# Attention with a routed MLP on one core: the last 20 score steps taken two at a time

## The chip, the cores and the metric

The kernel runs on one core of a Trainium2 chip. The metric is the device time of one execution in microseconds (us). The kernel before took 1442.85 us (median of 3 runs, 1442.76 to 1443.87).

## What is computed

```python
x = A_x                                              # 1 x 2048 x 512
g = sigmoid((x * gate_w).sum(-1, keepdims=True))
# a: 32 heads of 16 channels over 2048 tokens
q, k, v = heads(x @ wqkv)
p = softmax(q @ k.T * 16 ** -0.5)
a = merge(p @ v) @ wo
# b: the 2 tokens with the highest r = B_x @ w_r go through a SwiGLU MLP, times sigmoid(r), added to B_x
b = B_x + scatter(sigmoid(r_sel) * ((silu(x_sel @ w_gate) * (x_sel @ w_up)) @ w_down))
out = g * a + (1 - g) * b
```

Nearly all the work is the attention: 32 heads, each with a 2048 x 2048 score matrix.

## The kernel before, in words

**Units and steps.** The heads are taken in 16 pairs, and each pair in two halves of the queries (1024 each): 32 units. A unit goes through the 2048 keys in 16 blocks of 128, so there are 512 steps (`STEPS`). One step computes, transposed, the scores of 128 keys against 1024 queries for two heads: four *pieces* of S^T of 128 x 512, each one matmul into one PSUM bank (`s_piece`, L624), followed by an exp on ScalarE that writes a quarter of the SBUF tile `P` (L625). Which head a piece belongs to is `j` (rows 64 j and up of the K and Q tiles, 50 rows each), which half of the queries is `c`. The block P V of a step (`av_mm`, L633) is four column tiles of 32 accumulating into the one bank `av`; each of its four matmuls runs as two, so the trace shows eight. P V of step s - 2 is issued behind the pieces of step s. The tile `P` has three buffers.

**PSUM.** Eight banks: `st` (three, taken in rotation), `fl` (one), `mxa` (one tile of two banks), `mxb` (one), `av` (one). During the main part `mxa` and `mxb` hold the products from which VectorE takes row maxima (`m_piece`, L556 and L560). These run out before the steps do, and the last 20 steps (492 to 511) are driven by a plain loop, L922 to L930. There, the fourth piece of a step (c = 1, j = 0) goes to `mxb` and the other three to `st`.

**What the plain loop issues for a step.** `run_late`; the four pieces with their exps; P V of step s - 2; one entry of the generator `fills`; then `end_step(s)`, which runs what is due at that step in the table `fill`. Every engine takes its instructions in the order in which they are issued here. Two kinds of due work matter:

- *Output products* (`wo_last`, L534): three matmuls of 512 columns into the bank `fl` (L481), then `finish` on VectorE (L529), which reads `fl` and adds into `acc`. Products 8 to 15 (tokens of the second half, 96 rows) come from `fills` at steps 497 to 504, products 0 to 5 (128 rows, followed by a store to HBM, L532) from `end_step` at steps 506 to 511.
- *Pieces of the last heads' normalisation*: `n_last` (GpSimd, L679), `split_last` (cast on VectorE L524, subtraction on GpSimd L525) at steps 494, 495, 503 and 504; `l_cols` at 498 and `l_rows` at 499 (PE into `mxa`, L684 and L693, with VectorE L686, L688 and L695 behind them), `last_rows` at 500 (four DMAs, L700). Product 8 needs the first result of `split_last` of the second half, product 0 that of the first half.

P V of step 495 ends unit 30, whose sum VectorE copies out of `av` (L644). Steps 512 and 513 issue P V of 510 and 511 only. Then comes `tail`: the last unit's normalisation, its output products and the last ten stores.

Of the kernel before, what the change touches and what calls it, by code (L numbers as in the profile page):

```python
# [10 lines left out]
AF = mybir.ActivationFunctionType  # L11
# [9 lines left out]
KT = S // 128  # L21
VW = DH + 1
LEAD = 21
STEPS = UNITS * KT
# [9 lines left out]
def gated_mix(ctx: ExitStack, tc: tile.TileContext, xT, x, wqkv, wo, w_rg, w_gate, w_up, w_down,  # L34
              consts, pos, out):
    nc = tc.nc
# [10 lines left out]
    def st_tile(shape=(128, 512)):  # L47
        return psum.tile(list(shape), F32, tag="st", name="st", bufs=3)
# [4 lines left out]
    def mxa_tile():  # L53
        return psum.tile([128, 2, 512], F32, tag="mxa", name="mxa", bufs=1)

    def mxb_tile(shape=(128, 512)):
        return psum.tile(list(shape), F32, tag="mxb", name="mxb", bufs=1)
# [119 lines left out]
    def run_late():  # L177
        for f, a in late:
            f(*a)
        late.clear()  # L180
# [57 lines left out]
    def load_k(pair):  # L238

        g, r = divmod(pair * 32, 128)  # L240
        for j in range(2):
            o = (g * 128 + r + 16 * j) * S
            t = Kx[pair % 2].bitcast(F32)
            nc.sync.dma_start(t[64 * j:64 * j + 32, :], ap(qk_scr["k"], o, [[S, 16], [D * S, 2], [1, S]]).bitcast(F32))
            nc.sync.dma_start(t[64 * j + 32:64 * j + 48, :], ap(qk_scr["k"], o, [[S, 16], [1, S]]).bitcast(F32))

    def load_q(u):

        pair, half = divmod(u, 2)
        g, r = divmod(pair * 32, 128)  # L250
        n = S // 2
        for j in range(2):
            o = (g * 128 + r + 16 * j) * S + half * n
            t = Qx[u % 3].bitcast(F32)
            nc.sync.dma_start(t[64 * j:64 * j + 32, :], ap(qk_scr["q"], o, [[S, 16], [0, 2], [1, n]]).bitcast(F32))
            nc.sync.dma_start(t[64 * j + 32:64 * j + 48, :], ap(qk_scr["q"], D * S + o, [[S, 16], [1, n]]).bitcast(F32))
# [287 lines left out]
    MX, P, AV = {}, {}, {}  # L544
# [69 lines left out]
                p0 = 32 * b + 16 * j  # L614
                nc.sync.dma_start(q[:, :, 32 * b:32 * b + 32].bitcast(F32), r[p0:p0 + 16, :].bitcast(F32))  # L615

    def s_piece(s, j, c):
        u, kt = divmod(s, KT)
        if s not in P:
            P[s] = ring.tile([128, 4, 512], F32, tag="P", name="P", bufs=3)  # L620
        k = Kx[(u // 2) % 2][64 * j:64 * j + 50, kt * 128:kt * 128 + 128]
        q = Qx[u % 3][64 * j:64 * j + 50, c * 512:c * 512 + 512]
        ps = mxb_tile() if s > STEPS - LEAD and c == 1 and j == 0 else st_tile()
        nc.tensor.matmul(ps, k, q, start=True, stop=True)  # L624
        nc.scalar.activation(P[s][:, 2 * j + c, :], ps, AF.Exp)  # L625

    def av_mm(s):
        u, kt = divmod(s, KT)
        if kt == 0:
            AV[0] = av_tile()  # L630
        for ct in range(4):
            h = (u // 2) * 2 + ct // 2
            nc.tensor.matmul(AV[0][32 * ct:32 * ct + 32, :], V[:, kt, h * VW:h * VW + 32], P[s][:, ct, :],  # L633
                             start=kt == 0, stop=kt == KT - 1)
        del P[s]
# [3 lines left out]
    def av_out(u):  # L639
        pair, half = divmod(u, 2)  # L640
        g, pp = divmod(pair, 4)
        o = o_tile("o", [128, 512])
        if STEPS > u * KT + KT + 2 > STEPS - LEAD:
            nc.vector.tensor_copy(o, AV[0])  # L644
        else:
            nc.scalar.activation(o, AV[0], AF.Copy)
        if pair == PAIRS - 1:
            AV[u] = o
            return
        if u % 8 == 0:  # L650
            Lt[g] = ring.tile([128, 128], F32, tag="Lt", name="Lt", bufs=1)
        for ct in range(4):
            j, c = divmod(ct, 2)
            q0 = c * 512
            r = pp * 32 + j * 16
            if g < 3:
                d = a_scr[g * 128 + r:g * 128 + r + 16, half * 1024 + q0:half * 1024 + q0 + 512]
            else:
                d = last_n[half][r:r + 16, q0:q0 + 512]
            nc.sync.dma_start(d, o[32 * ct:32 * ct + 16, :])  # L660
            p = r + half * 8 + c * 4
            nc.sync.dma_start(Lt[g][p:p + 4, :], o[32 * ct + 16:32 * ct + 17, :])
# [91 lines left out]
    fill, now = {}, [0]  # L754

    def at_step(s, f, *a):
        fill.setdefault(s, []).append((f, a))

    def end_step(s):
        now[0] = s  # L760
        for f, a in fill.pop(s, []):
            f(*a)
# [28 lines left out]
    def slots():  # L791
        for w, nb in order:
            yield from proj(1, w, nb, 3)
        late.append((split_w, (2,)))
        at_step(now[0] + 4, load_w, 3)
        x_rows()
        yield
        for w, nb in order:
            yield from proj(2, w, nb, 3)
        for n, (w, nb) in enumerate(order):  # L800
            yield from proj(3, w, nb, 3)
            if w == "q":
                for i in range(4):
                    at_step(now[0] + i + 1, load_ff, ("gate", "up")[i // 2], (w_gate, w_up)[i // 2],
                            ("xh", "xl")[i // 2], nb, i % 2)
        yield from ff_in("gate")
        for j in range(4):
            at_step(now[0] + 2 * j, load_down, j)
        ff_t(0, "gate")
        yield  # L810
        yield from ff_in("up")
        ff_t(1, "up")
        late.append((ff_act, ()))
        at_step(now[0] + 3, ff_h)
        at_step(now[0] + 3, load_wo)
        for c in range(4):
            at_step(now[0] + 6 + c, split_wo, c)
        yield
        yield
        yield from ff_down()  # L820
        ff_sum()
        last_tiles()
        s = now[0]
        for nb in range(4):
            at_step(s + 5 + 2 * nb, load_acc, nb)
        for t in range(16):
            at_step(s + 11 + t, acc_scale, t)
        at_step(s + 1, load_at, 0, (0, 1))
        at_step(s + 4, split_at, 0, (0, 1))
        yield from wait(s + 8)  # L830
        yield from wo_groups((0, 1), (2,))
        assert now[0] > 3 * 8 * KT + 16
        yield from wo_groups((2,))
        yield from wait(STEPS - 15)
        for t in range(8, 16):
            wo_last(t, 96)
            yield

    fills = slots()
# [8 lines left out]
    def p_v(s):  # L848
        if not 0 <= s < STEPS:
            return  # L850
        av_mm(s)
        if s % KT < KT - 1:
            return
        u, s = s // KT, now[0]
        av_out(u)
        if u % 8 == 7 and u < 24:
            for i in range(8):
                at_step(s + 6 + i, l_out, u // 8, i)
        elif u == UNITS - 3:
            for i in range(8):  # L860
                at_step(s + 3 + i // 2, l_out, 3, i)
            for half in (1, 0):
                for q in range(2):
                    at_step(s + 10 - half, l_last, half, q)
                    at_step(s + 12 - half, n_last, half, q)
        elif u == UNITS - 2:
            at_step(s + 1, l_cols, u)
            at_step(s + 2, l_rows, u)
            at_step(s + 3, last_rows)

    def start_step(s):
        now[0] = s
        u = s // KT + 2
        if s % KT == 0 and u < UNITS:
            if u % 2 == 0 and u > 2:
                load_k(u // 2)
            load_q(u)

    count = dict(s=0, m=0, A=-2)
# [22 lines left out]
    while count["m"] < UNITS * EL:  # L902
        run_late()
        for o in ORDER:
            if o == "s":
                s, i = divmod(count["s"], 4)
                if i == 0:
                    start_step(s)
                s_piece(s, i % 2, i // 2)
                count["s"] += 1  # L910
                if i == 3:
                    end_step(s)
            elif o == "m":
                m_next()
            elif o == "A":
                if count["A"] < 0:
                    parts_next(3)
                p_v(count["A"])
                count["A"] += 1
            else:  # L920
                next(fills, None)
    for s in range(count["s"] // 4, STEPS + 2):  # L922
        run_late()
        if s < STEPS:
            start_step(s)
            for i in range(4):
                s_piece(s, 1 - i % 2, i // 2)
        p_v(s - 2)
        next(fills, None)
        end_step(s)  # L930
    end_step(STEPS + 2)
    assert next(parts, 0) == 0 and not fill and next(fills, 0) == 0, fill
    tail()
# [31 lines left out]
```

## Time and profile before

| | us |
|---|---|
| median of the runs | 1442.85 |
| the profiled execution | 1443.71 |
| its span, first to last instruction | 1441.9 |
| PE busy / VectorE busy / ScalarE busy / GpSimd busy | 1426.5 / 1300.1 / 1168.7 / 302.5 |
| start of step 492, the first of the plain loop | 1372.76 |
| start of the last two P V blocks | 1424.41 |

A row of the timeline gives the start in the span, the length, the engine, the source line, the operation with out<-in, shapes and count (neighbours of one kind are merged), and in brackets how long the engine had been idle and who released it. PEld is the load of the stationary operand, which runs beside PE's matmuls. Matmul lengths contain the latency of the array, so the distance between starts tells what a matmul costs in a stream.

### The profile page before, as it was taken

How to read it: one execution, taken by the hardware profiler on the slowest of the kernel's cores; microseconds unless marked ns; L12 is line 12 of the kernel's file. 1: busy time of each engine (PE TensorE's matmuls, PEld its weight loads, DVE VectorE, ACT ScalarE, POOL GpSimd, SP SyncE). 2: the span in 40 equal slices, each digit the busy share in tenths (PEclk: the TensorE clock that was granted, in tenths of full speed). 3: DMA queues.
4: the chain of work that ended last, by engine and by line, in shares of the span. 5: the costliest groups of instructions: out<-in, count | busy, mean ns of one | idle time of the engine just before them, and what ended most of it. 6: DMA issues, size and time to landing. Idle time of an engine off the chain costs nothing.

```text
span 1441.9 us, 24169 instructions
## 1 busy us (share of the span) xinstructions
PE 1426.5 (99%) x9141; PEld 631.9 (44%) x9141; DVE 1300.1 (90%) x1541; ACT 1168.7 (81%) x2262; POOL 302.5 (21%) x321
## 2 busy tenths in 40 slices
PE   8999999999999999999999999999999999999998
PEld 5654444444444444444444443434444444444434
DVE  5779999999999999999999999999999999999933
ACT  4468888888888888888888888888888888888874
POOL 3652000112000001200001100033832222233220
PEclk9999999999999999999999999999999999999999
DMA  8702021212214121312222342314213121111003
GB/s 265 195 21 64 20 52 31 53 45 41 53 53 107 61 53 31 67 31 64 57 81 52 98 104 70 86 42 130 73 31 68 35 53 27 32 31 38 25 17 117
DMA packets 53475, 92.71 MB, mean 64 GB/s; under 512 B 12972, under 2 KB 24300, under 8 KB 51856
## 3 DMA queue, kind: packets, MB, share of 16 engines
q1 hardware_dynamic: 53264, 91.17, 24.4%
q8 instruction: 72, 1.18, 0.4%
q14 instruction: 43, 0.35, 0.1%
q0 software_dynamic: 96, 0.01, 0.0%
HBM read 63.64 MB, written 28.56 MB: 64 GB/s over the span
## 4 chain that ended last, share of the span: by engine, by line
PE 95%; DMA 2%; DVE 1%; SPq 1%; ACT 0%; issue 0%; POOL 0%; DVEq 0%; POOLq 0%; ACTq 0%
PE av L633 35%; PE st L624 23%; PE mxa L556 12%; PE mxb L556 10%; PE fl L150 6%; PE fl L481 4%; PE st L268 3%; DMA xs<-xT 1%; PE mxa L583 1%; DVE Mr L560 1%; DMA wvs<-wqkv 1%; PE fl L372 0%; DVE acc L529 0%; PE st L150 0%; ACT P L625 0%; SPq L615 0%
## 5 line engine op out<-in xcount | busy, mean ns | idle before, releaser
L625 ACT ACTIVATE P<-st 128x512 f32<-128x512 f32 x2028 | 1064.5, 599 | 206.9 <-PE st L624 112.9
L560 DVE TENSOR_REDUCE Mr<-mxa 128x2 f32<-128x1024 f32 x655 | 794.9, 1214 | 3.8 <-PE mxa L556 3.5
L633 PE MATMUL av<-P,V 128*32 128x512 f32 x4096 | 545.5, 605 | 0.0
L624 PE MATMUL st<-Qx,Kx 50*128 50x512 f32 x2028 | 536.2, 443 | 2.0 <-ACT P L625 2.0
L560 DVE TENSOR_REDUCE Mr<-mxb 128x1 f32<-128x512 f32 x654 | 451.9, 691 | 63.5 <-PE st L624 18.1
L624 PEld LDWEIGHTS st<-Qx,Kx 50*128 50x128 f32 x2028 | 274.6, 184 | 234.6 <-ACT P L625 215.0
L556 PE MATMUL mxb<-Kx,Qx 48*128 48x512 f32 x654 | 325.3, 497 | 0.0
L556 PE MATMUL mxa<-Kx,Qx 48*128 48x512 f32 x1310 | 296.7, 420 | 1.2 <-DVE Mr L560 1.2
L556 PEld LDWEIGHTS mxb<-Kx,Qx 48*128 48x128 f32 x654 | 119.5, 183 | 273.7 <-DVE Mr L560 254.4
L556 PEld LDWEIGHTS mxa<-Kx,Qx 48*128 48x128 f32 x1310 | 125.1, 183 | 52.2 <-DVE Mr L560 10.3
L633 PEld LDWEIGHTS av<-P,V 128*32 128x32 f32 x4096 | 80.9, 108 | 140.3 <-issue 134.7
L186 POOL TENSOR_SCALAR ev<-pe 128x512 fp32r<-128x512 f32 x24 | 35.7, 1490 | 321.3 <-ACT pe L184 321.3
L74 POOL TENSOR_SCALAR hl<-m 128x16 fp32r<-128x16 f32 x32 | 8.1, 253 | 441.1 <-DVE m L599 441.0
L448 POOL TENSOR_TENSOR acc<-acc,w 128x512 f32<-128x512 f32 x32 | 41.0, 1281 | 185.8 <-ACT w L447 171.6
L150 PE MATMUL fl<-xh,wh 128*128 128x512 f32 x96 | 42.9, 447 | 0.0
L150 PE MATMUL fl<-xh,wl 128*128 128x512 f32 x96 | 40.4, 421 | 0.0
L529 DVE SCALAR_TENSOR_TENSOR acc<-fl,gg,acc 128x512 f32<-128x512 f32 x15 | 11.3, 750 | 26.6 <-PE fl L481 26.6
L481 PE MATMUL fl<-woh,ahl 128*128 128x512 f32 x96 | 35.1, 447 | 0.0
L588 DVE TENSOR_REDUCE Mr<-mxa 128x2 f32<-128x1024 f32 x21 | 25.7, 1223 | 9.8 <-PE mxa L583 9.8
L150 PE MATMUL fl<-xl,wh 128*128 128x512 f32 x96 | 32.6, 421 | 0.0
L187 POOL TENSOR_TENSOR ev<-pe,ev 128x512 fp32r<-128x512 f32 x24 | 30.8, 1283 | 2.0
L270 ACT ACTIVATE V<-st 128x512 f32<-128x512 f32 x16 | 9.6, 598 | 25.4 <-PE st L268 25.4
(177 smaller groups left out, 781.4 us busy)
## 6 DMA issues: line engine op xcount, KB each, us to landing
Qx<-q_scr SPq DMA_DIRECT2D x62, 128.0 KB
Kx<-k_scr SPq DMA_DIRECT2D x30, 256.0 KB
k_scr<-ev SPq DMA_DIRECT2D x14, 512.0 KB
q_scr<-ev SPq DMA_DIRECT2D x14, 512.0 KB
xs<-xT SPq DMA_DIRECT2D x16, 256.0 KB
xn<-x SPq DMA_DIRECT2D x4, 1024.0 KB
Qx<-hr SPq DMA_DIRECT2D x256, 2.0 KB
acc<-x_scr SPq DMA_DIRECT2D x4, 1024.0 KB
```

The lines of the kernel that those rows point to most:

```text
L150: nc.tensor.matmul(ps, a[:, i, c, :], b[nb][:, c, :], start=n == 0, stop=n == 11)
L186: nc.gpsimd.tensor_scalar(ev[:, 0], t, 1.0, None, op0=OP.mult)
L187: nc.gpsimd.tensor_sub(ev[:, 1], t, ev[:, 0].bitcast(F32))
L268: nc.tensor.matmul(ps, a[nb][:, c, sl], b[:, c, :], start=c == 0 and n == 0, stop=c == 3 and n == 2)
L448: nc.gpsimd.tensor_add(a, a, w)
L481: nc.tensor.matmul(ps, a[:, sl], b[:a.shape[0], c, :], start=first and n == 0, stop=last and n == 2)
L556: nc.tensor.matmul(dst, Qx[u % 3][64 * j:64 * j + 48, t * 128:t * 128 + 128], Kx[(u // 2) % 2][64 * j:64 * j + 48, c * 512:c * 512 + 512], ...
L560: nc.vector.tensor_reduce(Mr[:, g0:g0 + (2 if r == 1 else 1)], MX[r - 1], axis=AX.X, op=OP.max, negate=True)
L588: nc.vector.tensor_reduce(*r, axis=AX.X, op=OP.max, negate=True)
L624: nc.tensor.matmul(ps, k, q, start=True, stop=True)
L625: nc.scalar.activation(P[s][:, 2 * j + c, :], ps, AF.Exp)
L633: nc.tensor.matmul(AV[0][32 * ct:32 * ct + 32, :], V[:, kt, h * VW:h * VW + 32], P[s][:, ct, :], start=kt == 0, stop=kt == KT - 1)
```

## The change

```diff
+    exps = []
+
+    def s_exp(s, i, ps):
         if s not in P:
             P[s] = ring.tile([128, 4, 512], F32, tag="P", name="P", bufs=3)
+        nc.scalar.activation(P[s][:, i, :], ps, AF.Exp)
+
+    def s_piece(s, j, c, ps=None, defer=False):
+        u, kt = divmod(s, KT)
         k = Kx[(u // 2) % 2][64 * j:64 * j + 50, kt * 128:kt * 128 + 128]
         q = Qx[u % 3][64 * j:64 * j + 50, c * 512:c * 512 + 512]
-        ps = mxb_tile() if s > STEPS - LEAD and c == 1 and j == 0 else st_tile()
+        if ps is None:
+            ps = mxb_tile() if s > STEPS - LEAD and s % 2 == 0 and c == 1 and j == 0 else st_tile()
         nc.tensor.matmul(ps, k, q, start=True, stop=True)
-        nc.scalar.activation(P[s][:, 2 * j + c, :], ps, AF.Exp)
+        if defer:
+            exps.append((s_exp, (s, 2 * j + c, ps)))
+        else:
+            s_exp(s, 2 * j + c, ps)
...
-    for s in range(count["s"] // 4, STEPS + 2):
+    s = count["s"] // 4
+    while s < STEPS + 2:
+
         run_late()
+        n = 1 + (s % 2 == 0)
         if s < STEPS:
-            start_step(s)
-            for i in range(4):
-                s_piece(s, 1 - i % 2, i // 2)
-        p_v(s - 2)
-        next(fills, None)
-        end_step(s)
+            two = mxa_tile() if n == 2 else None
+            for k in range(n):
+                start_step(s + k)
+                for i in range(4):
+                    s_piece(s + k, 1 - i % 2, i // 2, two[:, i] if k and i < 2 else None, bool(k))
+        for k in range(n):
+            p_v(s + k - 2)
+            for f, a in exps:
+                f(*a)
+            exps.clear()
+        for k in range(n):
+            now[0] = s + k
+            next(fills, None)
+            end_step(s + k)
+        s += n
```

The plain loop starts at step 492 and takes steps in pairs. A pair issues its eight pieces first, then P V of the two steps two back, then the due work of both steps: `fills` and `end_step` of the even one, `fills` and `end_step` of the odd one. Of the eight pieces the first three go to `st`, the fourth to `mxb`, the fifth and sixth to the two banks of `mxa`, the seventh and eighth to `st` again. The exps of the first four are issued with their pieces; those of the last four are issued after the first of the two P V blocks, since their `P` buffer is the one which that block reads.

More of the change, by code (lines that the diff above doesn't have):

```diff
@@ L615, in m_rows @@
                 nc.sync.dma_start(q[:, :, 32 * b:32 * b + 32].bitcast(F32), r[p0:p0 + 16, :].bitcast(F32))
-    def s_piece(s, j, c):
-        u, kt = divmod(s, KT)
+    exps = []
+    def s_exp(s, i, ps):
         if s not in P:
             P[s] = ring.tile([128, 4, 512], F32, tag="P", name="P", bufs=3)
+        nc.scalar.activation(P[s][:, i, :], ps, AF.Exp)
+    def s_piece(s, j, c, ps=None, defer=False):
+        u, kt = divmod(s, KT)
         k = Kx[(u // 2) % 2][64 * j:64 * j + 50, kt * 128:kt * 128 + 128]
         q = Qx[u % 3][64 * j:64 * j + 50, c * 512:c * 512 + 512]
-        ps = mxb_tile() if s > STEPS - LEAD and c == 1 and j == 0 else st_tile()
+        if ps is None:
+            ps = mxb_tile() if s > STEPS - LEAD and s % 2 == 0 and c == 1 and j == 0 else st_tile()
         nc.tensor.matmul(ps, k, q, start=True, stop=True)
-        nc.scalar.activation(P[s][:, 2 * j + c, :], ps, AF.Exp)
+        if defer:
+            exps.append((s_exp, (s, 2 * j + c, ps)))
+        else:
+            s_exp(s, 2 * j + c, ps)
     def av_mm(s):
```

## The prediction

> **What bounds the kernel now.** First the page: the chain that ended last, by engine.
>
> ```profile
> PE 95%; DMA 2%; DVE 1%; SPq 1%; ACT 0%; issue 0%; POOL 0%; DVEq 0%; POOLq 0%; ACTq 0%
> ```
>
> PE is 95% of the chain. The change touches only steps 492 to 511, so I read the timeline there. Step 508 is typical of a step with an output product:
>
> ```profile
> 1414.17 0.73 PE L624 MATMUL st<-Qx,Kx 50*128 50x512 f32 x3
> ...
> 1414.51 0.39 PE L624 MATMUL mxb<-Qx,Kx 50*128 50x512 f32 x1
> 1414.70 1.58 ACT L625 ACTIVATE P<-st 128x512 f32<-128x512 f32 x3 [0.50 <-PE st L624]
> ...
> 1414.83 1.07 PE L633 MATMUL av<-P,V 128*32 128x512 f32 x8
> ...
> 1415.83 0.74 PE L481 MATMUL fl<-woh,lahl 128*128 128x512 f32 x2
> 1416.15 0.62 ACT L625 ACTIVATE P<-mxb 128x512 f32<-128x512 f32 x1
> ...
> 1416.41 0.40 PE L481 MATMUL fl<-wol,lahl 128*128 128x512 f32 x1
> 1416.73 0.73 PE L624 MATMUL st<-Qx,Kx 50*128 50x512 f32 x3
> ...
> 1416.84 0.75 DVE L529 SCALAR_TENSOR_TENSOR acc<-fl,gg,acc 128x512 f32<-128x512 f32 x1 [1.82 <-PE fl L481]
> ```
>
> PE never rests: pieces from 1414.17, P V from 1414.83 (0.66), product from 1415.83 (1.00), next pieces at 1416.73 (0.90); 2.56 us in all. ScalarE had waited 0.50 us and VectorE 1.82 us. So PE's order is the bound. The boundaries below are the starts of the pieces, by steps:
>
> ```profile
> 1387.03:1390.38 3.35, 3.35 (x24) 1.99 (x23) 1.43 (x2) 2.06 (x4) 0.53 (x1) 1.00 0.01 2
> 1390.38:1393.82 3.44, 3.44 (x24) 1.99 (x23) 1.51 (x4) 2.06 (x4) 0.00 (x0) 1.00 0.00 0
> 1393.82:1398.94 5.12, 5.12 (x31) 1.88 (x30) 1.44 (x2) 4.08 (x8) 0.00 (x0) 1.00 0.13 29
> 1398.94:1404.07 5.13, 5.13 (x31) 1.88 (x30) 1.50 (x2) 4.15 (x9) 0.00 (x0) 1.00 0.00 0
> 1404.07:1408.29 4.22, 4.22 (x29) 1.40 (x28) 2.17 (x4) 3.23 (x8) 1.68 (x2) 1.00 0.00 0
> 1408.29:1411.60 3.31, 3.31 (x19) 1.20 (x15) 0.00 (x0) 2.89 (x6) 0.89 (x1) 1.00 0.00 0
> 1411.60:1414.16 2.56, 2.56 (x16) 0.94 (x15) 0.75 (x1) 2.03 (x4) 0.00 (x0) 1.00 0.27 102
> 1414.16:1419.30 5.14, 5.14 (x32) 1.89 (x31) 1.50 (x2) 4.14 (x9) 0.00 (x0) 1.00 0.27 102
> 1419.30:1424.41 5.11, 5.11 (x32) 1.88 (x31) 1.50 (x2) 4.12 (x9) 0.00 (x0) 1.00 0.29 106
> ```
>
> Each row is the stretch, its length, then busy time of PE, PEld, DVE, ACT and POOL, and the granted clock (1.00). They are steps 498, 499, 500-501, 502-503, 504-505, 506, 507, 508-509, 510-511.
>
> **What pairing saves on PE.** What does a second block cost directly behind one of its kind?
>
> ```profile
> 1424.41 1.92 PE L633 MATMUL av<-P,V 128*32 128x512 f32 x16
> ...
> 1424.86 0.13 PEld L633 LDWEIGHTS av<-P,V 128*32 128x32 f32 x4 [0.30 <-issue]
> ...
> 1425.29 0.13 PEld L633 LDWEIGHTS av<-P,V 128*32 128x32 f32 x4 [0.30 <-issue]
> ...
> 1432.90 0.39 PE L749 MATMUL st<-wz,onh 128*128 128x512 f32 x1
> ...
> 1433.12 0.39 PE L749 MATMUL st<-wz,onl 128*128 128x512 f32 x1
> ```
>
> The last two P V blocks already stand together: 1.92 us for 16 matmuls where 8 show 1.07, so the second adds 0.85, and a pair of blocks costs 1.00 + 0.85 = 1.85 instead of 2.00. Matmuls of 512 columns in a stream start 0.23 apart (1432.90, 1433.12), so a second product adds 0.69 instead of 0.90, and four more pieces (two at a time, since the two heads lie on different rows) 0.45 instead of 0.66. Without any wait a pair would cost PE 1.12 + 1.85 + 1.59 = 4.56 us against 5.13: 0.56 saved. The Trainium skill, TensorEngine Tiling (Array Packing), Key Properties, gives the reason: a change of tiling mode drains the engine. Pieces, P V and product are three modes, and the 0.15 to 0.21 that a block loses by standing alone agrees; by that rule alone the pair is 0.56 us faster (the third rival).
>
> **What pairing adds: two waits.** The first is in the pieces. The seventh and eighth go to the `st` banks of the first and second, so they wait for exps 1 and 2 of their own pair. How PE waits for an exp shows in step 493:
>
> ```profile
> 1373.30 1.57 ACT L625 ACTIVATE P<-st 128x512 f32<-128x512 f32 x3 [0.54 <-PE st L624]
> ...
> 1374.92 0.18 PEld L624 LDWEIGHTS st<-Qx,Kx 50*128 50x128 f32 x1 [0.31 <-ACT P L625]
> ...
> 1375.41 0.50 PE L624 MATMUL mxb<-Qx,Kx 50*128 50x512 f32 x1
> 1375.84 1.07 PE L633 MATMUL av<-P,V 128*32 128x512 f32 x8
> ```
>
> The third exp ended at 1374.87 and PE went on at 1374.92: 0.05. A single last piece holds P V off by 0.43 (1375.41 to 1375.84). In step 508 exp 1 starts 0.53 after the first piece, three exps take 1.58 at 0.60 each, so they start 0.49 apart and exp 2 ends at 0.53 + 0.49 + 0.60 = 1.62. The eighth piece then starts at 1.67 and P V at **2.10**, where the unstalled group would reach it at 1.12: a wait of 0.98, in a phase that cost 2 x 0.66 = 1.33 before. Behind the waiting piece on PE stand both P V blocks and the products. ScalarE in turn waits for P V of step s - 2 (it frees the buffer of exps 5 to 8): 2.10 + 1.07 + 0.05 = 3.22 after the pair's start; exp 8 ends at 5.3.
>
> The second wait is in the products. Both use the single bank `fl`. In step 508 the product starts at 1415.83, `finish` at 1416.84 and ends at 1417.59; with the same 0.05 the bank is free **1.82** after the product's start. Before, the next step's pieces and P V (1.66) lay in between and the wait was covered; now nothing does, and the second product starts at 1.82 instead of 0.81 and takes 0.90 more: 2.72 against 1.81. Behind it stand the next pair's pieces, and so ScalarE.
>
> A pair with two products: 2.10 + 1.85 + 2.72 = **6.67 us** against 5.13, with exp 8 (5.3) done before the next pair starts. The bounds: the exp release cannot be under zero nor is it seen above 0.05 here, and the handover from VectorE is bounded by the same rows and, above, by the 0.15 to 0.2 of a block's start; so a pair lies between 6.5 and 6.9.
>
> **Where the first three pairs go.** Steps 492 to 497 have no product before product 8, and that one waits for GpSimd:
>
> ```profile
> 1369.71 3.04 ACT L625 ACTIVATE P<-st 128x512 f32<-128x512 f32 x6 [0.42 <-PE st L624]
> ...
> 1372.76 0.50 PE L624 MATMUL st<-Qx,Kx 50*128 50x512 f32 x2
> ...
> 1376.65 0.67 ACT L625 ACTIVATE P<-mxb 128x512 f32<-128x512 f32 x1
> 1376.84 0.73 PE L624 MATMUL st<-Qx,Kx 50*128 50x512 f32 x3
> ...
> 1378.79 0.73 PE L624 MATMUL st<-Qx,Kx 50*128 50x512 f32 x3
> ...
> 1384.98 0.50 PE L481 MATMUL fl<-woh,lahl 96*128 96x512 f32 x1
> 1385.04 2.52 POOL L525 TENSOR_TENSOR lahl<-an,lahl 96x512 fp32r<-96x512 f32 x2
> ...
> 1386.37 0.50 PE L481 MATMUL fl<-woh,lahl 96*128 96x512 f32 x1 [0.88 <-POOL lahl L525]
> ...
> 1387.03 0.73 PE L624 MATMUL st<-Qx,Kx 50*128 50x512 f32 x3
> ```
>
> Before, a step without a product took some 2 us (1376.84 to 1378.79), set by ScalarE's four exps, 0.48 apart in a run (six in 3.04 us) and up to 0.67 long. Now exps 5 to 8, and 1 and 2 of the next pair, run on end to end; the eighth piece waits for the last of them, then P V must end before exp 5 can start: 5 x 0.48 + 0.65 + 0.05 + 0.43 + 1.12 = 4.65 us for a pair, some 0.6 more than before. Started at 1372.76, the pairs have exp 5 at 1375.98, 1380.63 and 1385.28, so P V of the third at 1384.16 and product 8 at 1386.01, 1.03 late. But its second matmul waits for GpSimd until 1386.37 in any case; now PE would come to it 0.34 behind the first (an estimate, from 1414.17 to 1414.51 above), at 1386.35. So step 498 starts at 1387.03 as before: **zero**, with no cover to spare, and up to 0.5 if I have the exps too short. GpSimd's own chain hangs on DMAs issued earlier and stays.
>
> **The pair 498-499** has `l_cols` behind product 9 and `l_rows` behind product 10:
>
> ```profile
> 1389.50 0.95 PE L684 MATMUL mxa<-cst,o 128*128 128x4 f32 x8
> ...
> 1390.84 0.43 DVE L688 COPY rx<-r 128x512 f32<-128x512 f32 x1
> ...
> 1392.84 1.05 PE L693 MATMUL mxa<-cst,rx 128*128 128x128 f32 x8
> ```
>
> Here `l_cols` (0.88 to the next pieces at 1390.38) covers most of the wait for `fl`: product 9 at 1387.03 + 3.95 = 1390.98, `l_cols` at 1391.79, product 10 at 1392.80 (`fl`), `l_rows` at 1393.61 (`rx` is ready 1.77 after `l_cols` begins plus 0.05, the same moment), pieces at +0.98 = 1394.59: 7.56 against 6.79.
>
> **The sum**, after minus before, from the rows of stretches: 498-499 +0.77; 500 to 503 two pairs, 13.34 - 10.25 = +3.09; 504-505 with one product, 2.10 + 1.85 + 0.90 = 4.85 - 4.22 = +0.63; 506-507 6.67 - 5.87 = +0.80 (step 506 had waited for exps before); 508-509 +1.53; 510-511 +1.56. Together **+8.4 us**. The last two P V blocks, adjacent before too, and the tail keep their 17.5 us.
>
> At nothing I cost what moves with `end_step`: the four DMAs of `last_rows` go out about 0.8 later, and their reader, VectorE's cast of the first half, now stands behind product 14 near 1408; cover is over 10 us, and product 0 comes only at 1416.7, so GpSimd's 1.3 us lies in between. The six stores move later with their products, but the last keeps its distance to the tail's. SP's queue holds nothing else here.
>
> The profiled execution took 1443.71, 1.8 over its span and 0.86 over the median of the runs; it would become 1452.1. On the median's footing: 1442.85 + 8.4 = **1451.2 us**.
>
> **The rivals.** (1) Only the pieces wait; the products do not, if the second found another bank. Against: `fl` is one bank. Less 0.91 in five pairs and 0.13 in 498-499: +3.7, 1446.5 us. (2) Only the products wait: if the seventh and eighth pieces found free banks. Less 0.98 in seven pairs: +1.5, 1444.4 us, which cannot be told from no change. It is also how the change could fail to do what it says: "six banks" holds only as far as these two pieces do not stall. (3) The other side: PE's changeovers decide. If both waits of a pair together stay under 0.56 us, the pair gains; with none, 498-499 -0.34, four plain pairs -2.24, 504-505 -0.35, 506-507 -1.31: -4.2, 1438.6 us. For it speaks that PE is the bound and that ScalarE needs only 8 x 0.48 = 3.8 us of 4.56; against it that the waits come to 0.98 + 1.13 = 2.1. (4) Slower still: about 2 us of rest in each pair lowers PE's granted clock. At half speed a pair's 4.56 of PE work becomes 9.1 plus the wait for `finish`, some 10 us, +3.5 on each of six pairs more: near 1472 us. Against: the clock column reads 1.00 in all stretches above, the first of them right behind the 0.88 us of rest that ended at 1386.37. The Trainium skill, TensorE: Matmul & The Clock Gate, section "A second HAM failure mode: psum-queue depth-cycling", tells of a kernel whose short rests between groups, from cycling through PSUM banks, made the clock swing; no run here shows it yet.
>
> **Numbers.** Both waits: 0.82; rival 1: 0.05; rival 2: 0.05; rival 3: 0.05; rival 4: 0.03. The forecast's own range is 1449.3 to 1453.5: 0.2 either way on six pairs, and up to 0.5 in the first three. The range given reaches down to rival 1 and leaves 2, 3 and 4 out: 1446.0 to 1454.0. About 0.2% (2.9 us) is what a measurement tells from no change: slower 0.90 (forecast, rivals 1 and 4), same 0.05 (rival 2), faster 0.05 (rival 3).
>
> **What would show it.** In the profile after: pairs of 6.7 us from step 500 on; in each, the seventh and eighth matmul of L624 released by ACT, P V 2.1 us after the first piece, and the second product's first matmul released by DVE L529 about 1.8 after the first's; 16 matmuls of P V in 1.9 us; step 498 still at 1387.0, released by POOL. It is wrong if PE runs through the eight pieces in 1.1 us, if the second product follows the first within 0.8, or if step 498 starts later than 1387.5.

## The result, and the profile after

The changed kernel takes 1455.76 us (median of 6 runs; one of them, at 7006.74 us, lies far from all others and is left out of the ratio) against 1443.36 for the kernel before on the same chips: ratio 1.0077, 95% interval 1.0065 to 1.0089, some 11 us slower by the ratio. Slower was forecast, at 1451.2; the measured time lies above the range, which ended at 1454.0.

The profiled execution took 1455.82 us, its span 1454.0. The pairs by the starts of their pieces (length, then busy PE, PEld, DVE, ACT, POOL, and the granted clock), from step 492 on; the last row is what follows the last product:

```profile
1373.02:1376.97 3.95, 3.73 (x29) 1.27 (x25) 1.81 (x2) 2.73 (x6) 2.11 (x2) 1.00 0.03 6
1376.97:1381.69 4.72, 4.25 (x29) 1.45 (x25) 0.00 (x0) 4.03 (x9) 0.00 (x0) 1.00 0.15 50
1381.69:1388.99 7.30, 6.83 (x32) 2.13 (x28) 0.69 (x1) 5.43 (x11) 4.98 (x4) 0.77 0.06 23
1388.99:1396.71 7.72, 7.45 (x47) 4.25 (x46) 2.94 (x5) 4.13 (x8) 0.00 (x0) 1.00 0.00 0
1396.71:1403.42 6.71, 5.75 (x31) 2.24 (x30) 1.44 (x2) 4.13 (x8) 0.00 (x0) 1.00 0.10 23
1403.42:1411.68 8.26, 7.20 (x33) 2.53 (x32) 1.50 (x2) 4.13 (x8) 0.00 (x0) 0.79 0.00 0
1411.68:1416.53 4.85, 4.63 (x28) 1.75 (x27) 1.08 (x2) 3.63 (x8) 1.27 (x1) 1.00 0.00 0
1416.53:1423.21 6.68, 5.84 (x32) 2.30 (x32) 1.83 (x3) 4.63 (x10) 1.28 (x1) 1.00 0.01 5
1423.21:1429.87 6.66, 5.60 (x31) 2.24 (x30) 1.50 (x2) 4.13 (x8) 0.00 (x0) 1.00 0.21 79
1429.87:1436.54 6.67, 5.61 (x31) 2.25 (x31) 1.50 (x2) 4.13 (x8) 0.00 (x0) 1.00 0.22 81
1436.54:1453.97 17.43, 11.33 (x63) 7.83 (x62) 9.46 (x17) 1.77 (x4) 0.00 (x0) 0.97 0.47 178
```

Four of the five pairs with two plain products take 6.66 to 6.71 us; forecast were 6.67. Two rows stand out by their clock column, 0.77 and 0.79. The timeline of a pair at full clock, 508-509, answers to the step 508 shown of before:

```profile
1423.21 0.73 PE L630 MATMUL st<-Qx,Kx 50*128 50x512 f32 x3
...
1423.55 0.39 PE L630 MATMUL mxb<-Qx,Kx 50*128 50x512 f32 x1
1423.74 1.57 ACT L622 ACTIVATE P<-st 128x512 f32<-128x512 f32 x3 [1.84 <-PE st L630]
1423.77 0.40 PE L630 MATMUL mxa<-Qx,Kx 50*128 50x512 f32 x2
...
1424.39 0.98 PE L630 MATMUL st<-Qx,Kx 50*128 50x512 f32 x2 [0.22 <-ACT P L622]
...
1425.30 1.93 PE L642 MATMUL av<-P,V 128*32 128x512 f32 x16
...
1427.16 0.73 PE L481 MATMUL fl<-woh,lahl 128*128 128x512 f32 x2
...
1427.73 0.40 PE L481 MATMUL fl<-wol,lahl 128*128 128x512 f32 x1
1428.16 0.75 DVE L529 SCALAR_TENSOR_TENSOR acc<-fl,gg,acc 128x512 f32<-128x512 f32 x1 [4.09 <-PE fl L481]
1428.97 0.30 PEld L481 LDWEIGHTS fl<-woh,lahl 128*128 128x128 f32 x2 [1.28 <-DVE acc L529]
1428.97 0.74 PE L481 MATMUL fl<-woh,lahl 128*128 128x512 f32 x2 [0.84 <-DVE acc L529]
```

Both waits are there and carry the names they were given: the seventh piece is released by ACT (1424.39), P V starts 2.09 us after the first piece, and the second product, released by DVE L529, 1.81 us after the first. ScalarE had waited 1.84 us before its first exp: it is not the bound.

What the forecast lacked stands in the two rows with the low clock. PE alone, in stretches of 3.41 us:

```profile
1377.79:1381.20 3.41, 3.27 (x23) 1.00 0.15 53
1381.20:1384.62 3.42, 2.95 (x20) 1.00 0.17 63
1384.62:1388.03 3.41, 3.41 (x16) 0.50 0.00 0
...
1401.68:1405.10 3.42, 2.36 (x12) 1.00 0.00 0
1405.10:1408.51 3.41, 3.41 (x17) 0.50 0.00 0
1408.51:1411.92 3.41, 2.57 (x16) 1.00 0.00 0
1418.75:1422.16 3.41, 2.71 (x19) 1.00 0.00 0
```

Twice in this loop PE's granted clock falls to 0.50 for 3.41 us, each time behind a stretch in which PE had rested. (In the kernel before, the clock reads 1.00 from step 492 to the tail; both kernels have such a stretch near 33 us and one among the last stores.) What it costs is seen in the P V blocks that fall into it:

```profile
1384.55 3.62 PE L642 MATMUL av<-P,V 128*32 128x512 f32 x16
...
1405.81 3.23 PE L642 MATMUL av<-P,V 128*32 128x512 f32 x16
```

Sixteen matmuls take 3.62 and 3.23 us instead of 1.93. The first stretch costs 1.7 us (3.62 less 1.92), the second 1.6 (8.26 less 6.67). From the start of step 492 to the last two P V blocks the kernel before took 1424.41 - 1372.76 = 51.65 us, this one 1436.54 - 1373.02 = 63.52: 11.87 more, of which by this working 3.3 are the clock and 8.6 the rest; forecast were 8.4.

### The profile page after: what moved, and what is told of

It reads as the page before. It is cut to its first block, busy times and chain, and to the rows that moved or that the text cites. A ratio compares the mean times of both kernels' runs of the same rounds, so it can differ in the third digit from the quotient of the medians.

```text
span 1454.0 us, 24180 instructions
## 1 busy us (share of the span) xinstructions
PE 1432.7 (99%) x9141; PEld 634.9 (44%) x9141; DVE 1299.3 (89%) x1541; ACT 1169.2 (80%) x2262; POOL 302.5 (21%) x321
## 4 chain that ended last, share of the span: by engine, by line
PE 95%; DVE 1%; DMA 1%; ACT 1%; SPq 1%; issue 0%; DVEq 0%; ACTq 0%
PE av L642 35%; PE st L630 23%; PE mxa L556 12%; PE mxb L556 10%; PE fl L150 6%; PE fl L481 4%; PE st L268 3%; ACT P L622 1%; DMA xs<-xT 1%; DVE acc L529 1%; PE mxa L583 1%; DMA wvs<-wqkv 0%; PE fl L372 0%; DVE Mr L560 0%; PE st L150 0%
## 5 line engine op out<-in xcount | busy, mean ns | idle before, releaser
L529 DVE SCALAR_TENSOR_TENSOR acc<-fl,gg,acc 128x512 f32<-128x512 f32 x15 | 11.2, 750 | 35.4 <-PE fl L481 35.3
```

Source lines behind the costliest of these rows:

```text
L529: nc.vector.scalar_tensor_tensor(a, ps, gg[:, t:t + 1], a, op0=OP.mult, op1=OP.add)
```

## The experiments

The theory after the result: the two waits make 8.4 us as worked out, and the rest is half-speed stretches that PE's rests bring on. The rivals: the loss lies in one of the waits alone or in the order of the exps; and the half-speed stretches have nothing to do with the rests.

**A second bank for the products.**

```diff
 def wo_last(t, k):
-        ps = fl_tile()
+        ps = mxb_tile() if now[0] % 2 == 0 and now[0] != 504 else fl_tile()
```

> The even step's product goes to mxb (free by then), the odd one's stays in fl; all else as in the changed kernel. Theory of the two waits: the second product now follows the first by 0.81 us instead of 1.82, a pair with two products shrinks from 6.67 to 5.54 us; five such pairs and 0.1 us in 498-499: 5.8 us less, about +2.6 us over the kernel before (1446) if the clock stays full, and up to 1.7 more for each half-speed stretch. The seventh and eighth piece still wait 1.0 us. Rival (the loss is in the pieces or in the order of the exps alone, the wait for fl being covered): same time as the changed kernel, near 1455. Clock: if rest on PE brings the half-speed stretches, there are fewer than in the changed kernel, the pair's rest falling from 2 us of 6.7 to 1 us of 5.5; if they come at random, two in a profile as often as before.

Measured: 1447.5 us, ratio 1.0015 (1.0005 to 1.0025), +2.2 us by the ratio and +3.1 by the medians, where +2.6 was expected. The pair 506-507 in its profile:

```profile
1417.12 0.73 PE L481 MATMUL mxb<-woh,lahl 128*128 128x512 f32 x2
1417.69 0.40 PE L481 MATMUL mxb<-wol,lahl 128*128 128x512 f32 x1
1417.92 0.62 PE L481 MATMUL fl<-woh,lahl 128*128 128x512 f32 x2
```

The second product follows after 0.80 us, and the pairs from 500 on with two products take 5.55 to 5.61. The wait for `fl` was real and cost what it was priced at here (5.54 a pair). One half-speed stretch is left, from 1384.91; the one in pair 502-503 is gone.

**The last two pieces behind P V.**

```diff
-                for i in range(4):
+                for i in range(4 - 2 * k):
                     s_piece(s + k, 1 - i % 2, i // 2, two[:, i] if k and i < 2 else None, bool(k))
         for k in range(n):
             p_v(s + k - 2)
...
+        if s < STEPS:
+            for i in (2, 3):
+                s_piece(s + 1, 1 - i % 2, i // 2)
```

> Pieces seven and eight move behind the two P V blocks; the products still share fl. Theory of the two waits: six pieces run through in 0.89 us, the other two cost 0.44 behind P V without a wait, a pair goes from 6.67 to 5.90 us (0.89 + 1.85 + 0.44 + 2.72), seven pairs: 5.4 us less, about +3 us over the kernel before (1446) at full clock. In the profile the second product still waits 1 us for VectorE's finish. Rival (the wait for the bank is hidden anyway, or ScalarE is the bound): no gain, or a loss from the extra changeover, 1455 or more.

Measured: 1447.88 us, ratio 1.0023 (1.0014 to 1.0032), +3.3 us by the ratio, +3.5 by the medians. Its pair 506-507:

```profile
1410.80 1.03 PE L630 MATMUL st<-Qx,Kx 50*128 50x512 f32 x3
...
1412.00 1.92 PE L642 MATMUL av<-P,V 128*32 128x512 f32 x16
1413.85 0.51 PE L630 MATMUL st<-Qx,Kx 50*128 50x512 f32 x2
1414.29 0.73 PE L481 MATMUL fl<-woh,lahl 128*128 128x512 f32 x2
...
1416.09 0.73 PE L481 MATMUL fl<-woh,lahl 128*128 128x512 f32 x2 [0.84 <-DVE acc L529]
```

The two pieces cost 0.44 us (1413.85 to 1414.29) and wait for nothing, while the second product still comes 1.80 after the first. Pairs 502-503 and 508-509 take 5.87 and 5.89 us (expected 5.90); 500-501 and 506-507, whose first six pieces wait as well, 6.28 and 6.18. In this profile the clock does not fall between step 492 and the tail, although the products still wait.

**Both.** The two edits above together.

> Both edits: products in two banks, pieces seven and eight behind P V. Theory of the two waits: with neither wait a pair with two products takes 0.89 + 1.85 + 0.44 + 1.59 = 4.77 us, ScalarE needs 3.85; the gains add up: 8.4 - 5.8 - 5.4 = -2.8 us, about 1440.5, faster than the kernel before by 0.2%. No half-speed stretch, as PE rests less than in the kernel before. Rival (PE's order is not the only bound; eight exps and the buffer of P hold the pair at 5.1 us or more): equal to the kernel before, 1443, or above.

Measured: 1442.21 us, ratio 0.9979 (0.9970 to 0.9988): 3 us faster than the kernel before by the ratio, 2.2 by the medians. From step 492 to the last two P V blocks the profiles show 54.8 us with the second bank, 55.4 with the two pieces moved and 50.1 with both, against 60.2 of the changed kernel, each less what its half-speed stretches cost (1.7, none, 1.5 and 3.3). So the edits save 5.4, 4.8 and together 10.1 us: the gains add up, these two waits are the loss, and PE's changeovers decide where they are gone, as the third rival had it. The pairs with two products take 4.76 to 5.15 us. The expectation was wrong in one point: there is a half-speed stretch, from 1388.94, behind product 8's wait for GpSimd, which has become longer here (1.47 us instead of 0.88).

**The rests filled.** Idle matmuls repeat work whose result is overwritten or never read; `again` issues a piece's matmul once more. The edit adds 52 of them (28, 4 and 20), not the 42 that the expectation counts: the profile has 9193 matmuls instead of 9141.

```diff
+                    if k and i == 2 and s >= 498:
+                        for _ in range(2):
+                            for m in range(2):
+                                again(s + k, 1 - m, two[:, m])
                     s_piece(s + k, 1 - i % 2, i // 2, two[:, i] if k and i < 2 else None, bool(k))
+                    if not k and i == 0 and s in (494, 496):
+                        for _ in range(2):
+                            again(s, 1, two[:, 0])
...
         finish(t, ps)
+        if now[0] in (500, 502, 506, 508, 510):
+            spare = mxb_tile()
+            for _ in range(4):
+                nc.tensor.matmul(spare, ah[:k, tt * 128:tt * 128 + 128], wop[0][:k, 3, :], start=True, stop=True)
```

> The changed kernel plus 42 idle matmuls: where PE waits, it repeats matmuls whose results are overwritten or never read (four between the sixth and seventh piece from pair 498 on, four into mxb between the two products, two behind the first piece of pairs 494 and 496). They fit into the waits, so at full clock the time is the changed kernel's, 8.4 us over the kernel before plus at most 1, about 1452. Theory (half-speed stretches come from PE's rest in a window): the clock stays full in every run, mean 0.998, and the kernel is 2 to 4 us faster than the changed one although it does more. Rival (the stretches have another cause): two stretches as before, and 1455 to 1457.

Measured: 1453.55 us, ratio 1.0056 (1.0042 to 1.0069). Then once more beside the changed kernel on one chip:

> The changed kernel unaltered, on the same chip as the next one. Theory (rest brings half-speed stretches): times spread from 1452 (none) to 1457 (three), a stretch in the profile behind a stretch of 3.4 us in which PE rested most, and the mean is 1 to 3 us above the kernel with the rest filled. Rival: it lies with it, inside both intervals.

> The changed kernel with its waits filled by idle matmuls, as above, on the same chip as the changed kernel. Theory: no half-speed stretch between the start and the last matmul, every time within 1.5 us of the others, ratio 1.0055 to 1.006, below the changed kernel's. Rival: stretches as in the changed kernel and the same mean.

Measured: the changed kernel 1454.56 us, 1.0067 (1.0047 to 1.0087), from 1451.2 to 1457.68; the filled one 1454.77, 1.0070 (1.0053 to 1.0087), from 1453.58 to 1455.76. In time the two cannot be told apart, against the expectation. Their profiles can. The changed kernel's has the same two stretches again (1384.62 and 1405.10); neither of the filled kernel's has one between step 492 and the tail. In the first of them, pairs 496-497 and 502-503:

```profile
1381.08:1386.99 5.91, 5.88 (x34) 2.23 (x30) 0.69 (x1) 5.22 (x11) 4.52 (x4) 1.00 0.08 29
...
1401.42:1408.13 6.71, 6.71 (x40) 3.36 (x39) 1.50 (x2) 4.13 (x8) 0.00 (x0) 1.00 0.00 0
```

They took 7.30 and 8.26 before the filling, with fewer matmuls. From step 492 to the last two P V blocks it is 60.74 and 60.90 us instead of 63.52 and 63.49. About half of that is given back at the end: from the start of the last `finish` to the end of the span it is 5.4 and 5.6 us instead of 4.1, in the stores to HBM; why, no run here settles. In the second profile step 492 also starts 0.87 us later than in the changed kernel's beside it, and the half-speed stretch near 30 us, which all versions have, lasts 6.83 us there instead of 3.41.

So I filled less, only between the products (the second part of the edit):

> The changed kernel with idle matmuls (results never read) only between the two products of five pairs, 20 in all; the waits of the pieces stay. Theory (a half-speed stretch follows a stretch of 3.4 us in which PE rested most): the stretch in pair 502-503 does not come, that near 1385 (rest among the pieces of 494 to 497) may come as before; the pairs from 500 on take 6.7 us each, the time is 1.6 us below the changed kernel's with both stretches, about 1453. Rival (the stretches come at fixed times, or by chance): 502-503 takes 8.3 us as before.

Measured: 1452.64 us, ratio 1.0059 (1.0046 to 1.0072). Its pairs 496-497, 500-501 and 502-503:

```profile
1379.49:1386.73 7.24, 6.77 (x31) 2.37 (x28) 0.69 (x1) 5.43 (x11) 5.00 (x4) 0.76 0.07 23
...
1394.46:1401.17 6.71, 6.59 (x36) 2.99 (x35) 1.44 (x2) 4.13 (x8) 0.00 (x0) 1.00 0.11 23
1401.17:1407.88 6.71, 6.44 (x36) 3.00 (x35) 1.50 (x2) 4.13 (x8) 0.00 (x0) 1.00 0.00 0
```

The stretch at the place that was left as it was came again, the one at the filled place did not: 6.71 us instead of 8.26. The end is 4.1 us, as in the changed kernel. In time this kernel cannot be told from the changed one either (the intervals overlap); it is the profiles that show the cause. The stretch among the pieces of 494 to 497 came in all five profiles that leave these rests as the changed kernel has them (twice the changed kernel, the second bank, this one, and the changed kernel of the next experiment) and in neither that fills them; the one in pair 502-503 came in all three that leave both of its waits, and in none that fills or removes one. The rival left is that the 3.41 us windows lay elsewhere by chance. Counted in steps of 3.413 us from the stretches of each profile, one begins 2.06 and 1.70 us before step 492 in the changed kernel, 2.20 in the first filled profile and 1.50 in this one: near enough the same. So the rests bring the stretches on, at these two places.

**GpSimd's order.** In front of the subtractions that product 8 waits for stand two multiplications which wait for a DMA. They are issued three steps later:

```diff
-                    at_step(s + 12 - half, n_last, half, q)
+                    at_step(s + (11 if half else 15), n_last, half, q)
```

This edit was made to the version with both edits, to the kernel before and to the changed kernel:

> As the run with both edits, and the two multiplications of n_last for the first half are issued three steps later on GpSimd (step 496 instead of 493), so that the subtractions product 8 needs no longer queue behind a DMA. Theory: product 8 does not wait, step 498 starts some 2 us earlier than with both edits (24 exps at 0.48 from 1373.3 on instead of GpSimd's 1387), 1438.5 to 1439.5, ratio 0.996 to 0.997; no half-speed stretch behind step 497, since the rest there is gone. Rival (something else holds step 498, the exps or the DMA of the rows): no gain over both edits, 0.998.

> The kernel before with the same two multiplications issued later, nothing else. Theory: product 8's wait for GpSimd goes (2.05 us from its first matmul to the next pieces, 0.90 for an unstalled product), 1.15 us less, ratio 0.999; fewer half-speed stretches too. Pairing without waits is then worth the difference to the run with both edits and this order, 2 to 3.5 us. Rival (the gain in that run was GpSimd's order alone): this one comes out as fast.

> The changed kernel with the two multiplications of n_last for the first half issued three steps later, as in the run of the kernel before with that order. Theory of the first three pairs (they lose about 1 us to the exps, and product 8's wait for GpSimd hid it): here nothing hides it, and the order of GpSimd, worth 1.1 us to the kernel before, is worth nothing at full clock: from step 492 to step 498 14.2 us or more, where the kernel before with that order took 13.15. Rival (the first three pairs lose nothing): 13.2 us, and the time falls by 1 us against the changed kernel. A half-speed stretch among them would add up to 1.7 us; that is read off the clock column.

Measured: 1440.68 us, 0.9972 (0.9963 to 0.9982) with both edits; 1442.22, 0.9986 (0.9977 to 0.9996) for the kernel before; 1453.82, 1.0069 (1.0051 to 1.0087) for the changed kernel. Steps 492 to 497, pair by pair, first of the kernel before with the new order, then of the changed kernel with it:

```profile
1374.56:1378.64 4.08, 4.08 (x28) 1.18 (x24) 1.82 (x2) 3.54 (x8) 3.72 (x4) 1.00 0.03 7
1378.64:1382.72 4.08, 4.08 (x29) 1.35 (x25) 0.00 (x0) 4.03 (x9) 1.02 (x1) 1.00 0.13 36
1382.72:1387.71 4.99, 4.99 (x32) 1.83 (x29) 0.69 (x1) 4.51 (x9) 2.55 (x2) 1.00 0.16 51
```

```profile
1371.63:1375.58 3.95, 3.74 (x28) 1.27 (x24) 1.81 (x2) 2.72 (x6) 3.59 (x4) 1.00 0.03 6
1375.58:1380.30 4.72, 4.25 (x28) 1.45 (x24) 0.00 (x0) 4.03 (x9) 1.15 (x1) 1.00 0.14 48
1380.30:1387.56 7.26, 6.79 (x32) 2.13 (x29) 0.69 (x1) 5.43 (x11) 2.53 (x2) 0.76 0.06 24
```

The kernel before gains 1.1 us in the third pair (4.99 after 6.11), as expected. The changed kernel gains nothing: 15.93 us for the three pairs, as without the edit (15.97), and the rival's 13.2 is out. At full clock it would be some 14.2 (less the 1.7 of a stretch, an estimate from the first one above), which is what was expected. So the first three pairs do lose about 1 us. That GpSimd can hide it is seen where no half-speed stretch falls among them, in the filled kernel (its second profile; step 492 starts at 1373.54):

```profile
1386.25 2.51 POOL L525 TENSOR_TENSOR lahl<-an,lahl 96x512 fp32r<-96x512 f32 x2
...
1386.93 1.15 PE L481 MATMUL fl<-woh,lahl 96*128 96x512 f32 x2
...
1387.57 0.19 PEld L481 LDWEIGHTS fl<-woh,lahl 96*128 96x128 f32 x1 [0.46 <-POOL lahl L525]
```

Product 8 starts 13.39 us after step 492, 1.17 later than in the kernel before, but its second matmul still waits for GpSimd, and step 498 starts 14.70 us after step 492 (14.58 in the first profile) against 14.27. In the changed kernel as it ran, PE at half speed came to product 8 only at 1388.10 and GpSimd was no longer waited for.

The version with both edits and the new order beats both kernels, 3 to 4 us below the kernel before (medians and ratio). Its profile has no half-speed stretch between step 492 and the tail, as expected, and step 498 starts 12.62 us after step 492 instead of 14.38 with both edits alone; its ratio lies just above the 0.996 to 0.997 that was expected. Pairing itself is worth the difference to the kernel before with the new order, 1.5 us by the medians and 2 by the ratios.

## Why the prediction was wrong, point by point

- **What bounds it, and the saving on PE: right.** P V of two steps takes 1.86 us (1425.30 to 1427.16; forecast 1.85), and with the waits taken out the kernel is faster, if by 2 to 3 us and not by the 4.2 of the third rival.
- **The wait in the pieces: right**, 2.09 us to P V against 2.10; moving the two pieces brought pairs of 5.87 and 5.89 us (5.90).
- **The wait for `fl`: right**, 1.81 us against 1.82; a second bank brought pairs of 5.55 to 5.61 us. The first rival had priced this wait at 0.91 a pair; the runs show 1.1, as the prediction's own 2.72 against 1.59 gives.
- **The first three pairs at nothing: right in its mechanism.** They lose about 1 us, which product 8's wait for GpSimd takes up but for 0.3 to 0.4 us where the clock stays full (the filled kernel). In the changed kernel's own profile the sign that the prediction set for itself came all the same: step 498 started at 1388.99, later than 1387.5 and not released by GpSimd, 1.7 us more for the three pairs, by the clock.
- **The pair 498-499:** 7.72 against 7.56: `l_rows` starts 0.14 behind the end of the copy into `rx` (1395.65 after 1395.51) where 0.05 was assumed, and takes 1.06 to the next pieces instead of 0.98.
- **The sum: near at full clock**, 8.6 against 8.4 by the working above. Two other readings give a little more: the two filled profiles, which have no half-speed stretch here, take 60.74 and 60.90 us, 9.1 and 9.3 more than before, with their idle matmuls in them; and the one execution of the changed kernel whose mean clock reads 1.0 took 1451.2 us, 8.9 above the fastest of the kernel before beside it (1442.3, clock 0.999). The forecast's own range, 1449.3 to 1453.5, does not come out of the two terms it names, which give 1450.0 to 1452.9; the measured time is outside either.
- **The step that failed is the fourth rival.** It asked only whether the clock would fall to half throughout (1472 us), found 1.00 in every row of before, and gave that 0.03. What happens is between: one or two single stretches of 3.41 us, each worth 1.6 to 1.7 us, which the sum and the range put at nothing. A term of 0 to 3.4 us was missing from the range: with it, it would have reached to about 1457 and held the median. Of the 4.6 us between forecast and median this is 3.3 in the profiled execution; 0.5 more is the kernel before, which took 1443.36 beside the changed one. The kernel before does not seem free of it either: its executions in the second series run from 1442.3 us at a mean clock of 0.999 to 1449.36 at 0.994. The row that I set against it, a rest of 0.88 us without a fall in the clock, was one rest among steps that keep PE busy, while the change puts about 2 us of waiting into each 6.67.
- The Trainium skill, TensorE: Matmul & The Clock Gate, section "What's actually happening", says that the clock is set by free-running windows of 4096 cycles, 3413 ns. The trace agrees: the stretches last 3.41 us and start 20.48 us apart (1384.62, 1405.10), six times 3.413. The practical rule in the closing table of the same page of the Trainium skill (section "Why this matters for your kernels") is to leave no rest above about 3 us between bursts. Keeping to it was not enough here: in the two stretches before the clock fell PE was busy for 2.95 and 2.36 of 3.41 us by the profile, and no single rest of PE was longer than 0.84 us. The section of the Trainium skill on cycling through PSUM banks, cited in the prediction, comes nearer to what happened.

Open: how much rest it takes. A stretch with 2.57 us busy and one with 2.71 were not followed by a fall, one with 2.95 was, so the busy time of the profile does not give the threshold. The pairs from 506 on, whose products have 128 rows instead of 96, have the same waits and saw no fall. What the matmuls occupy of the array may count; no run here tests it. Nor is a single rest enough: with the two pieces moved, product 8 waited 1.39 us for GpSimd and the clock stayed at 1.00, with both edits it waited 1.47 and the clock fell. Open too: the filled kernel's longer end, and why it is not faster in time.

## What to carry to other kernels

Before two blocks are put side by side, follow each bank they share through its reader: what lay between them (here 1.66 us of other work) was what covered that reader, and the changeover saved (0.56 us a pair as worked out) is small against it. Here pairing paid once each block of the pair had a bank that was free, even at the price of one more changeover (4.76 us at best instead of 6.67). And a wait put on PE can cost more than its length: rests that recur brought one or two half-speed stretches here, so price one or two of these as a term of their own.

## What was not expected of the hardware

- In the changed kernel PE's clock fell to 0.50 for 3.41 us at a time with rests of at most 0.84 us; 20 idle matmuls in the rests kept it at 1.00 in one place (6.71 us instead of 8.26 for a pair) and 52 in both.
- The kernel with the 52 took 5.4 and 5.6 us from the start of the last `finish` to its end instead of 4.1, with the same ten stores; with 20 it took 4.1.
